# Attention loop reordered: projections one group ahead, assembly, memory update and output projection cut up among the QK steps, private PSUM banks, and five copies moved between ScalarE and VectorE

## The chip, the cores and the metric

One core of a Trainium2 chip. The metric is the device time of one execution in microseconds (us), as the median of several runs. The program on one core has executions that agree within some tenths of a per cent; runs more than 1.5% above the fastest of the same kernel are marked slow and are not used for ratios. Engines: PE (TensorE matmul; PEld is its weight load), ACT (ScalarE), DVE (VectorE), POOL, SP. Each engine is given its own list of instructions, in program order, and the engines wait for one another by semaphores.

## The reference, cut to what matters

```python
# x: 2048 x 640 bf16.  32 heads of 20; 4 segments of 512 rows.
for s in range(4):
    p = softmax(q_s k_s^T * scale + mask)     # causal within the segment
    a_dot = p @ v_s
    a_mem = (phi(q_s) @ M) / (phi(q_s) @ z + 1e-6)
    o_s = g * a_mem + (1 - g) * a_dot
    M, z = M + phi(k_s)^T v_s, z + sum(phi(k_s))
a = concat(o_s) @ wo
out = gate * a + (1 - gate) * b               # b: a 2D FFT filter of x ("part B")
```

`phi(t)` is `t + 1` for `t > 0` and `exp(t)` otherwise, so the q and k projections are needed twice: as they are, for QK, and through phi. The memory (M, z) goes from segment to segment.

## The kernel before

The kernel first computes part B (to about 330 us), then v for all rows (to 381 us), and then runs a loop over 4 segments x 8 groups of four heads. Only this loop, and the v stage a little, is touched. Every operation is recorded in program order by one helper, which puts a semaphore wait in front of it where a buffer needs one; PSUM banks are such buffers and are always exclusive. The parts that matter (cut):

```python
def proj_group(s, g):                  # q into PSUM bank 6, k into bank 7
    for which, ..., bank in (("q", ..., 6), ("k", ..., 7)):
        5 matmuls of 128x512 -> bank
        dve: qT or kT <- bank                     # copy, bf16
        act: pq or pk <- exp(bank)
        dve: rq <- max(qT, 0);  pq <- min(pq, 1) + rq

def qk_unit(s, g, j):                  # j = 0..3: keys of block j, queries from block j on
    for pair in range(2):              # two heads at a time; banks 0..5: three pair slots
        b0 = 2 * (pairctr[0] % 3)
        2 matmuls, 32 rows, N = 512 - 128 j;  2 mask matmuls 128x128
        act: expT <- exp(banks b0, b0 + 1)

def assembly(s, g):                    # bank 6 + g % 2 and bank 7 - g % 2
    PV: 40 matmuls of 22 columns;  4 matmuls pq x Mz_bf;  8 small dve operations -> o_sb

def m_update(s, g):                    # bank 6 + g % 2
    pe: 4 transposes of pk;  act: pkT <- bank;  4 matmuls pkT x v
    dve: 4 x (Mz_acc += bank; memset);  act: Mz_bf <- Mz_acc

def out_proj(s, i):                    # banks 6 and 7
    pe: 5 transposes of o_sb;  act: oT <- bank;  10 matmuls;  dve: outt;  dma

for s in range(NSEG):
    proj_group(s, 0)
    for ui, (g, j) in enumerate(units):
        if j == 0:
            if g + 1 < NG: proj_group(s, g + 1)
            if s <= 2: m_update(s, g)
            if pending_out: out_proj(*pending_out.pop(0))
        qk_unit(s, g, j)
        ...                            # assembly(s, g) two units after the group's last QK
    ...                                # rest of the assemblies; then four output tiles are pending
```

So one group is: projection of the next group, memory update, perhaps an output tile, all through banks 6 and 7, and then four QK steps.

## Time and profile before

| | us |
|---|---|
| median of 12 runs | 893.71 (891.36 to 895.69) |
| first QK matmul of the loop (timeline) | 390.9 |
| mean of a group, first QK to next first QK, 31 intervals | 15.2 |
| mean granted PE clock in the loop (0.5 or 1.0 at any moment) | 0.67 |

The page of the kernel before: busy time of the engines; busy tenths of PE and ACT and the granted PE clock in tenths, in 40 slices; and the shares of the chain of work that ended last.

```profile
span 893.4 us, 10954 instructions
...
PE 599.0 (67%) x4314; PEld 279.0 (31%) x4314; DVE 397.5 (44%) x1050; ACT 326.1 (37%) x530; POOL 16.6 (2%) x46
...
PE   0500799706967664867787776778677768786894
...
ACT  0494012201211113245455343455244355354661
...
PEclk9855599957987876976655757665668665669757
...
PE 54%; DVE 24%; ACT 14%; issue 4%; SPq 2%; DMA 1%; DVEq 0%; ACTq 0%
```

The loop begins at slice 17. PE is at 6 to 8 tenths there (9 once, and 4 in the last slice), ACT at 2 to 6 (1 in the last), and the clock row stands mostly at 5 to 7. DVE is busy 44% of the span. No engine is full. The next two fences are the waits of ACT and of PE within the loop: who waited for whom, us in total, times, longest.

```profile
ACT pq L922 <- DVE qT L921: 75.7, 30, 6.3
ACT expT L953 <- PE psum L270: 63.7, 57, 3.9
ACT Mz_bf L1022 <- DVE Mz_acc L1020: 55.9, 24, 2.5
```

```profile
PE psum L270 <- ACT pkT L1010: 32.5, 24, 2.1
PE psum L270 <- ACT expT L953: 22.2, 32, 1.8
PE psum L1008 <- ACT pk L922: 17.6, 9, 2.4
```

These are chains between engines. The timeline shows one of them (start us, us, engine, operation, and in brackets the idle time before it and who ended it):

```profile
712.38 1.26 PE L270 MATMUL psum<-xT,wk_pad 128*128 128x512 bf16 x5
...
712.60 0.69 DVE L921 CAST qT<-psum 128x512 bf16<-128x512 f32 x1 [1.89 <-PE psum L270]
713.32 0.60 ACT L922 ACTIVATE pq<-psum 128x512 bf16<-128x512 f32 x1 [2.39 <-DVE qT L921]
...
715.85 0.59 ACT L1010 ACTIVATE pkT<-psum 128x512 bf16<-128x512 bf16 x1
...
716.50 0.33 PE L270 MATMUL psum<-vaug,pkT 128*128 128x88 bf16 x4 [2.12 <-ACT pkT L1010]
...
718.69 0.31 ACT L1022 ACTIVATE Mz_bf<-Mz_acc 128x128 bf16<-128x128 f32 x1 [2.25 <-DVE Mz_acc L1020]
718.91 1.01 ACT L953 ACTIVATE expT<-psum 128x1024 bf16<-128x1024 f32 x1
```

While the k projection runs (712.38) qT is copied by DVE (712.60), then follow the exp of q on ACT (713.32, after ACT had idled 2.39 us for qT), the same for k, the pkT copy of the memory update on ACT (715.85), for which the PE waits 2.12 us (716.50), and at last the Mz_bf copy (718.69).

The last view is the busy time in chosen windows (us; the columns are the engines' busy time with the number of instructions, then the clock). The first line is 60 us of the loop, the others are successive windows of 3.41 us:

```profile
395.00:455.00 60.00, 47.87 (x378) 21.00 (x379) 22.26 (x68) 31.77 (x54) 0.00 (x0) 0.61 0.00 1
722.64:726.06 3.42, 3.42 (x18) 1.35 (x19) 2.10 (x7) 1.91 (x4) 0.00 (x0) 0.50 0.00 0
726.06:729.47 3.41, 2.89 (x7) 0.76 (x5) 2.15 (x4) 0.60 (x1) 0.00 (x0) 0.50 0.00 0
729.47:732.88 3.41, 1.82 (x18) 0.92 (x18) 2.02 (x8) 1.19 (x2) 0.00 (x0) 1.00 0.00 0
732.88:736.30 3.42, 2.06 (x35) 1.18 (x36) 0.53 (x4) 2.65 (x4) 0.00 (x0) 0.50 0.00 0
```

The clock is 0.50 or 1.00 for a whole window and never between. The Trainium skill, "TensorE: Matmul & The Clock Gate", Part 1, says that the PE's clock is gated to half by default, that activity opens the gate, and that this is decided per window of about 3.4 us. The trace agrees: each change in it lies on one grid of 3.413 us.

### The profile page before, as it was taken

Reading aid. Unit: us, or ns where it says so; the run is one execution under the profiler, and the core shown is the slowest. Engines: PE = TensorE matmul, PEld = TensorE weight load, DVE = VectorE, ACT = ScalarE, POOL = GpSimd, SP = SyncE. Lnnn points to the kernel's source line nnn. Section 1 sums busy time; section 2 is a strip of 40 time slices with the busy share of each in tenths; the row PEclk is TensorE's granted clock in tenths of the full one; section 3 lists DMA queues with packets and bytes.
Section 4 is the critical chain, followed back from the end, with each engine's and each line's share of the span. In section 5 each row is a group of like instructions: output and inputs, shape, how many; then the busy total and the mean of one; then the engine's idle time right before and its main releaser. Section 6 shows DMA issues by size and latency. Waiting matters only on the chain.

```text
span 893.4 us, 10954 instructions
## 1 busy us (share of the span) xinstructions
PE 599.0 (67%) x4314; PEld 279.0 (31%) x4314; DVE 397.5 (44%) x1050; ACT 326.1 (37%) x530; POOL 16.6 (2%) x46
## 2 busy tenths in 40 slices
PE   0500799706967664867787776778677768786894
PEld 0400244303433322423333333333233333333442
DVE  0476513796243433243433434444524444535542
ACT  0494012201211113245455343455244355354661
POOL 5000000000000000010000000000000000000000
PEclk9855599957987876976655757665668665669757
DMA  9800000000000031000000000000000000000000
GB/s 234 143 0 0 0 1 1 1 0 0 1 1 1 0 111 37 1 1 1 1 1 1 8 8 8 8 1 1 0 16 8 8 1 1 1 15 8 9 1 30
DMA packets 29936, 15.00 MB, mean 17 GB/s; under 512 B 23228, under 2 KB 29884, under 8 KB 29884
## 3 DMA queue, kind: packets, MB, share of 16 engines
q1 hardware_dynamic: 27248, 11.01, 5.2%
q10 hardware_dynamic: 2636, 3.28, 1.1%
q8 instruction: 34, 0.56, 0.2%
q14 instruction: 18, 0.15, 0.1%
HBM read 5.90 MB, written 2.62 MB: 10 GB/s over the span
## 4 chain that ended last, share of the span: by engine, by line
PE 54%; DVE 24%; ACT 14%; issue 4%; SPq 2%; DMA 1%; DVEq 0%; ACTq 0%
PE psum L270 52%; ACT expT L953 4%; DVE pq L924 2%; DVE qT L921 2%; DVE kT L921 2%; ACT pq L922 2%; SPq L124 2%; DVE t L438 2%; ACT pkT L1010 2%; DVE Mz_acc L1019 1%; ACT pk L922 1%; ACT t L443 1%; ACT oT L1034 1%; DVE Mz_acc L1020 1%; DVE prod L613 1%
## 5 line engine op out<-in xcount | busy, mean ns | idle before, releaser
L953 ACT ACTIVATE expT<-psum 128x1024 bf16<-128x1024 f32 (+3 forms) x256 | 165.8, 707 | 67.8 <-PE psum L270 65.7
L270 PE MATMUL psum<-qT,kT 32*128 32x256 bf16 (+3 forms) x512 | 102.1, 395 | 22.5 <-ACT expT L953 22.2
L270 PE MATMUL psum<-maskT,ident 128*128 128x128 bf16 x512 | 92.7, 278 | 0.0
L270 PE MATMUL psum<-xT,wq_pad 128*128 128x512 bf16 x160 | 64.3, 558 | 8.9 <-DVE mtmp L999 6.9
L921 DVE CAST qT<-psum 128x512 bf16<-128x512 f32 x32 | 22.1, 690 | 72.2 <-PE psum L270 72.2
L270 PE MATMUL psum<-xT,wk_pad 128*128 128x512 bf16 x160 | 52.4, 471 | 2.6 <-ACT pk L922 2.6
L983 DVE RECIPROCAL rs<-psum 128x16 f32<-128x16 f32 x32 | 8.2, 258 | 101.6 <-PE psum L270 101.6
L270 PE MATMUL psum<-wo_sb,oT 128*128 128x512 bf16 (+1 forms) x160 | 41.6, 439 | 16.1 <-ACT oT L1034 16.1
L270 PEld LDWEIGHTS psum<-maskT,ident 128*128 128x128 bf16 x512 | 32.0, 105 | 59.1 <-issue 50.4
L922 ACT ACTIVATE pq<-psum 128x512 bf16<-128x512 f32 x32 | 19.1, 597 | 77.1 <-DVE qT L921 77.1
L270 PEld LDWEIGHTS psum<-qT,kT 32*128 32x128 bf16 x512 | 25.7, 97 | 67.5 <-ACT expT L953 32.9
L270 PE MATMUL psum<-x_sb,Jsel 128*128 128x512 bf16 (+1 forms) x16 | 6.7, 459 | 53.4 <-DVE xm L506 53.4
L1044 DVE SCALAR_TENSOR_TENSOR outt<-psum,g_sb,yk 128x512 bf16<-128x512 f32 (+1 forms) x32 | 17.6, 551 | 53.4 <-PE psum L270 52.8
L270 PE MATMUL psum<-vaug,expT 128*128 128x22 bf16 x1280 | 39.9, 180 | 0.0
L270 PEld LDWEIGHTS psum<-vaug,expT 128*128 128x128 bf16 x1280 | 39.4, 104 | 0.2
L270 PE MATMUL psum<-wv_aug,xT 128*128 128x512 bf16 (+1 forms) x160 | 28.4, 328 | 15.9 <-ACT gB L889 11.4
L270 PE MATMUL psum<-cC,Xlr 128*128 128x512 bf16 (+1 forms) x48 | 14.1, 344 | 34.5 <-DVE Xlr L634 34.5
L922 ACT ACTIVATE pk<-psum 128x512 bf16<-128x512 f32 x32 | 19.1, 597 | 46.6 <-DVE kT L921 46.6
L720 ACT ACTIVATE yk<-psum 128x512 bf16<-128x512 f32 (+1 forms) x16 | 6.8, 425 | 78.2 <-PE psum L270 78.2
L270 PE MATMUL psum<-vaug,pkT 128*128 128x88 bf16 x96 | 9.5, 239 | 32.5 <-ACT pkT L1010 32.5
L704 DVE TENSOR_SCALAR uvt<-psum,omg 128x512 f32<-128x512 f32 (+1 forms) x16 | 8.7, 546 | 49.7 <-PE psum L270 49.7
L270 PEld LDWEIGHTS psum<-xT,wk_pad 128*128 128x128 bf16 x160 | 19.4, 124 | 36.0 <-issue 23.9
(209 smaller groups left out, 916.7 us busy)
## 6 DMA issues: line engine op xcount, KB each, us to landing
x_sb<-in_A_x_dram SPq DMA_DIRECT2D x1, 2560.0 KB, 10.0
out_dram<-outt SPq DMA_DIRECT2D x16, 160.0 KB, 1.8
wst<-in_A_wq_dram ACTq DMA_DIRECT2D x1, 800.0 KB, 4.8
wst<-in_A_wk_dram ACTq DMA_DIRECT2D x1, 800.0 KB, 6.6
wo_sb<-in_A_wo_dram ACTq DMA_DIRECT2D x1, 800.0 KB, 8.2
wst<-in_A_wv_dram ACTq DMA_DIRECT2D x1, 800.0 KB, 4.6
xT<-in_A_x_dram SPq DMA_TRANSPOSE x5, 5.3
WrT<-in_B_w_r_dram SPq DMA_TRANSPOSE x3, 5.3
```

The source lines that it names most:

```text
L124: h = eng.dma_start_transpose(out_ap, in_ap)
L270: return e.matmul(out_ap, lhsT, rhs, start=start, stop=stop, tile_position=tile_position)
L438: self.run("dve", lambda e: e.scalar_tensor_tensor(gt[:, 0:n], zt[:, 0:n], -TWO23, u_t[:, 0:n], ALU.add, ALU.subtract), r=[tagz, tagu], w= ...
L443: self.run("act", lambda e: e.activation(at[:, 0:n], gt[:, 0:n], ACT.Abs), r=[tagg], w=[taga])
L613: self.run("dve", lambda e, xa=xa, wa=wa, slot=slot: e.tensor_tensor(pr[slot], xa, wa, ALU.mult), r=rX + rW, w=[f"prod{slot}"])
L921: self.run("dve", lambda e, o_ps=o_ps, dstT=dstT, g=g: e.tensor_copy(dstT[:, g, :], o_ps), r=[pb[bank]], w=[A(tn)])
L922: self.run("act", lambda e, o_ps=o_ps, dstP=dstP, g=g: e.activation(dstP[:, g, :], o_ps, ACT.Exp), r=[pb[bank]], w=[A(pn)])
L924: self.run("dve", lambda e, dstP=dstP, g=g, rb=rb: e.scalar_tensor_tensor(dstP[:, g, :], dstP[:, g, :], 1.0, rb[:, :], ALU.min, ALU.add), ...
L953: self.run("act", lambda e, in_ap=in_ap, out_ap=out_ap: e.activation(out_ap, in_ap, ACT.Exp, scale=SC), r=[pb[b0], pb[b0 + 1]], w=[A(f"{ex ...
L1010: self.run("act", lambda e, pt=pt: e.activation(pt[:, :, :], psbf[:, tb * 1024:tb * 1024 + 4 * P].rearrange("p (a b) -> p a b", b=P), ACT. ...
L1019: self.run("dve", lambda e, dst=dst, src=src: e.tensor_tensor(dst, dst, src, ALU.add), r=[pb[tb]], w=[A("Mz_acc")])
L1044: self.run("dve", lambda e, o_ps=o_ps, c0=c0, cw=cw: e.scalar_tensor_tensor(ot[:, c0:c0 + cw], o_ps, gsb[:, st:st + 1], yk[:, st, c0:c0 + ...
```

## The change

The intent is to keep ACT and PE fed all the time: the projection of the next group, q and k apart, is put between the QK steps of this one, the assembly and the memory update of the previous group and an output tile likewise, and this goes on across segment ends. Each user has its own banks: QK 0 to 3 (two pair slots in place of three), PV 4, Mz and transposes 5, q 6, k 7 (an output tile's matmuls borrow 6 and 4, the memory product 7). qT and kT are evacuated by ACT; pkT, oT and Mz_bf by DVE. oT is now tracked tile by tile and no longer as one buffer of four tiles. The core of the diff (cuts marked; renamed banks and debug lines left out):

```diff
-                eng = "act" if (st + ci) % 2 == 0 else "dve"      # v stage
-                if eng == "act":
+                if ci == 0:
...
-                self.run("dve", lambda e, ...: e.tensor_copy(dstT[:, g, :], o_ps), ...)
+            self.run("act", lambda e: e.activation(dstT[:, g, :], o_ps, ACT.Copy), ...)
...
-                b0 = 2 * (pairctr[0] % 3)
+            b0 = 2 * (pairctr[0] % 2)
...
-            self.run("act", lambda e, pt=pt: e.activation(pt[:, :, :], psbf[...], ACT.Copy), ...)
+            self.run("dve", lambda e: e.tensor_copy(pt[:, :, :], psbf[...]), ...)
...
-            self.run("act", ... e.activation(Mz_bf[nb][:, g, :], Mz_acc[:, g, :], ACT.Copy), ...)
+            self.run("dve", ... e.tensor_copy(Mz_bf[nb][:, g, :], Mz_acc[:, g, :]), ...)
...
+        groups = [(s, g) for s in range(NSEG) for g in range(NG)]
+        proj_full(0, 0)
+        for gi, (s, g) in enumerate(groups):
+            nxt, prv = ...                       # across segment ends
+            upd = prv is not None and prv[0] <= 2
+            qk_pair(s, g, 0, 0); qk_pair(s, g, 0, 1)
+            if prv: assembly(*prv); ...          # four output tiles pending at a segment's end
+            qk_pair(s, g, 1, 0); qk_pair(s, g, 1, 1)
+            if nxt: proj_mm(*nxt, "q"); proj_copy, proj_exp, proj_dve(*nxt, "q"); proj_mm(*nxt, "k")
+            qk_pair(s, g, 2, 0); qk_pair(s, g, 2, 1)
+            if pending_mm: out_mm(*pending_mm.pop(0), b512=6, b128=4)
+            if upd: m_update(*prv)               # transposes of pk, pkT
+            if nxt: proj_copy, proj_exp, proj_dve(*nxt, "k")
+            qk_pair(s, g, 3, 0); qk_pair(s, g, 3, 1)
+            if pending_out: out_tr(...); pending_mm.append(...)
+            if upd: m_update_b(*prv)             # pkT x v, Mz_acc, Mz_bf
+        ...                                      # last assembly; last four tiles through all eight banks
```

## The prediction

> **What bounds the kernel now.** Only the attention loop (382 to 870 us of 893; by the timeline) is changed. It runs 32 groups (segment, four heads) at about 15.3 us each. By the group view, a group needs ACT about 7.5 us (eight exps back to back took 5.02 us; two 512-column exps at 0.60 each; small copies), DVE about 9 us, PE about 8 us at full clock but 12.4 us at half clock (five 512-column matmuls 1.27 or 2.34 us; one head pair with its two masks 0.54 or 0.86 us). No engine is full: in the timeline the projection, its evacuation (CAST 0.69, exp 0.60), the pk transposes, the pkT copy, the Mz product and out_proj follow one another between groups. PE waits there about 5 us and ACT 4 to 7 us; ACT's waits for qT total 77 us, PE's for pkT and oT 49 us.
>
> Second bound: the clock. In the windows view it is 0.5 or 1.0 only, changing on a 3.41 us grid, mean about 0.65 in the loop. The Trainium skill, "TensorE: Matmul & The Clock Gate", Part 1, says that activity in such a window releases the throttle; the trace agrees. Adding matmul columns x rows/128 per grid window, nearly every window above about 0.38 of the full-rate array was followed by clock 1.0 and those below by 0.5. So idle gaps shorter than a window count too; 32-row QK, and PV with 22 columns, count little.
>
> **What the change does.** The projection moves one group ahead, q and k between j steps; assembly, memory update and out_proj are cut up among the QK steps of the next group, and go on across segment ends; every user has its own PSUM banks (QK keeps two pair slots instead of three). qT/kT evacuation goes from DVE (0.69) to ACT (about 0.6); pkT, oT and Mz_bf from ACT to DVE. Work is almost unchanged: ACT about 7.7 us per group, DVE 7.5 (9.4 with out_proj), PE 7.8 (9.7) at full clock. Nothing much is removed: the gain is overlap.
>
> **Cost.** Laying these durations along the new order by hand gives, at full clock, 8.8 us per group and 10.3 with out_proj: 298 us for the loop. I don't expect full clock. Between two projections lie 6.6 us of QK/PV/transposes whose activity is about 0.35 to 0.4, just at the threshold, so windows without a projection or out_proj will often turn the clock to 0.5, and a projection will turn it back. Expected: 10.5 us for plain groups, about 11.5 with out_proj, mean clock in the loop 0.7 to 0.8, 346 us in all, PE the bound. Fill 5 us; the tail shrinks from 23 to about 19 us because eight banks are used. Everything before 382 us is unchanged, but for 1 us in the vaug stage.
>
> 381 + 5 + 346 + 19 = 751 us. I say **750 us**, 80% range **710 to 798** (full clock throughout 701; half clock throughout about 825). Faster by over 2%: 0.95; within 2%: 0.03; slower: 0.02.
>
> **What would show it.** Groups view: DVE's wait qT<-PE and ACT's wait pq<-DVE vanish; PE's waits for pkT and oT shrink below 10 us each. Windows: PE busy over 90% in the loop; clock still flips in 3.41 us steps. Chain of waits: the DVE share falls, PE's grows, with ACT exp steps. Busy time of ACT and DVE about unchanged in total.
>
> **What would make it wrong.** The interleave keeps every window above the threshold: then 700 to 715. Or in-order queues couple badly: DVE late (pkT copy queued behind outt, Mz behind pk), PE waiting for two QK slots or bank 5: then groups of 12 to 13 us, about 800.

## The result, and the profile after

| | before | after |
|---|---|---|
| median, us | 893.71 (12 runs) | 720.42 (8 runs, 719.24 to 723.41) |
| ratio of fast runs | 1 | 0.8065 (95%: 0.8052 to 0.8079) |
| first QK matmul of the loop, us | 390.9 | 382.9 |
| 31 group intervals, us | 471.4 | 312.9 |
| last group's first QK to the end, us | 31.2 | 23.2 |
| mean clock in the loop | 0.67 | 0.87 |

A ratio is the mean time of one kernel's fast runs over the mean of the other's fast runs in the same rounds, so it is not quite the ratio of the medians quoted. Rows 3 to 5 are worked out from the start times of QK matmuls in the two traces; their differences, 8.0 + 158.4 + 8.0, make up the 174.4 us between the two profiled spans. By segment the intervals went from 118.9, 137.6, 133.0 and 81.9 us (7 intervals in the last) to 83.5, 82.1, 78.6 and 68.7 us. The last segment has no memory update, and there the old order lost least.

The same lines of the page after:

```profile
span 719.0 us, 11006 instructions
...
PE 521.9 (73%) x4314; PEld 260.2 (36%) x4314; DVE 369.6 (51%) x1048; ACT 335.2 (47%) x532; POOL 16.6 (2%) x46
...
PE   0510079995149768663687988899989999899986
...
ACT  0089301121003111102426677667877678768871
...
PEclk9999999998559987885797788889978999879976
...
PE 62%; DVE 17%; ACT 13%; issue 3%; SPq 2%; DMA 1%; DVEq 0%; ACTq 0%
```

PE's row is at 8 and 9 in the loop (slices 22 to 38), ACT's at 6 to 8. DVE's share of the chain fell and PE's grew. The waits of PE and of ACT in the loop, the same views as before:

```profile
PE psum L275 <- ACT pk L933: 11.7, 16, 0.8
PE psum L275 <- ACT expT L974: 5.6, 10, 1.1
...
PE psum L275 <- DVE pkT L1027: 0.8, 2, 0.4
```

```profile
ACT expT L974 <- PE psum L275: 52.4, 86, 1.7
ACT qT L928 <- PE psum L275: 22.4, 18, 1.3
```

PE's wait of 32.5 us for pkT is 0.8 us now, the wait of ACT for qT, 75.7 us, and for the Mz additions, 55.9 us, are gone; what ACT now waits for is the PE. Some PE lines of segment 2 (timeline):

```profile
575.53 1.52 PE L275 MATMUL psum<-wo_sb,oT 128*128 128x512 bf16 x10
576.89 0.39 PE L1025 MATMUL psum<-ident,pk 128*128 128x128 bf16 x4
...
578.42 0.45 PE L1052 MATMUL psum<-ident,o_sb 128*128 128x128 bf16 x5 [0.38 <-DVE pkT L1027]
578.71 0.32 PE L275 MATMUL psum<-vaug,pkT 128*128 128x88 bf16 x4
...
582.13 1.24 PE L275 MATMUL psum<-xT,wq_pad 128*128 128x512 bf16 x5
583.22 1.24 PE L275 MATMUL psum<-xT,wk_pad 128*128 128x512 bf16 x5
```

The output tile (575.53), the pk transposes (576.89), the o_sb transposes (578.42), the Mz product (578.71) and both projections (582.13, 583.22) stand in one stream, with QK steps and PV in the cut lines between them and one wait of 0.38 us. In the stretches that the kernel before spent waiting, QK steps now run.

The windows after: 60 us of segment 0, then four successive windows in it; and two windows in segment 2:

```profile
395.00:455.00 60.00, 54.70 (x532) 26.78 (x530) 26.48 (x91) 42.80 (x69) 0.00 (x0) 0.81 0.01 2
438.54:441.96 3.42, 3.42 (x10) 1.24 (x10) 0.77 (x2) 2.17 (x4) 0.00 (x0) 0.50 0.00 0
441.96:445.37 3.41, 2.59 (x23) 1.15 (x21) 1.41 (x3) 2.18 (x5) 0.00 (x0) 1.00 0.01 2
445.37:448.78 3.41, 2.98 (x58) 1.99 (x58) 2.44 (x11) 2.76 (x6) 0.00 (x0) 1.00 0.00 0
448.78:452.20 3.42, 3.42 (x11) 1.25 (x10) 0.67 (x3) 2.15 (x3) 0.00 (x0) 0.50 0.02 5
```

```profile
571.66:575.08 3.42, 3.42 (x23) 1.48 (x22) 3.04 (x11) 2.96 (x5) 0.00 (x0) 1.00 0.00 0
575.08:578.49 3.41, 3.03 (x30) 1.70 (x30) 2.25 (x5) 2.97 (x7) 0.00 (x0) 1.00 0.00 0
```

In segment 0 the clock goes half, full, full, half, again and again. A group there takes 10.2 us (the last six intervals: 10.20, 10.22, 10.22, 10.49, 10.17, 10.23), and three windows are 10.24 us: the loop has locked to the clock's grid. In segment 2 (the last two lines), where groups 1 to 4 carry an output tile, the clock stays full from 564.8 to 609.2 us, and three of these groups, though they have more work, take 9.62, 9.62 and 9.35 us.

### The profile page after: what moved, and what is told of

Its sections match the earlier page's. It is cut to its first block, busy times and chain, and to the rows that moved or that the text cites. A ratio compares the mean times of both kernels' runs of the same rounds, so it can differ in the third digit from the quotient of the medians.

```text
span 719.0 us, 11006 instructions
## 1 busy us (share of the span) xinstructions
PE 521.9 (73%) x4314; PEld 260.2 (36%) x4314; DVE 369.6 (51%) x1048; ACT 335.2 (47%) x532; POOL 16.6 (2%) x46
## 4 chain that ended last, share of the span: by engine, by line
PE 62%; DVE 17%; ACT 13%; issue 3%; SPq 2%; DMA 1%; DVEq 0%; ACTq 0%
PE psum L275 61%; ACT expT L974 3%; SPq L129 2%; DVE t L443 2%; ACT t L448 2%; DVE prod L618 1%; ACT kT L928 1%; ACT pk L933 1%; ACT vaug L908 1%; DVE thr L717 1%; DVE yk L711 1%; DVE uvt L709 1%; DVE xm L511 1%; DVE uvt L714 1%; ACT Sq L446 1%
## 5 line engine op out<-in xcount | busy, mean ns | idle before, releaser
L275 PE MATMUL psum<-qT,kT 32*128 32x256 bf16 (+3 forms) x512 | 83.5, 323 | 10.8 <-ACT expT L974 5.6
L275 PE MATMUL psum<-maskT,ident 128*128 128x128 bf16 x512 | 77.1, 235 | 0.0
L275 PE MATMUL psum<-xT,wq_pad 128*128 128x512 bf16 x160 | 58.8, 517 | 0.3 <-ACT vaug L908 0.3
L275 PE MATMUL psum<-wv_aug,xT 128*128 128x512 bf16 (+1 forms) x160 | 28.4, 328 | 15.3 <-ACT gB L894 11.4
L940 DVE TENSOR_SCALAR rq<-qT 128x512 bf16<-128x512 bf16 x32 | 10.4, 324 | 42.2 <-ACT qT L928 42.2
L556 ACT ACTIVATE XST<-psum 128x512 bf16<-128x512 f32 (+2 forms) x13 | 6.5, 499 | 52.2 <-PE psum L275 43.6
L928 ACT ACTIVATE qT<-psum 128x512 bf16<-128x512 f32 x32 | 19.1, 597 | 24.4 <-PE psum L275 23.8
L275 PE MATMUL psum<-Fr,Cq 128*128 128x128 bf16 (+1 forms) x128 | 29.9, 390 | 0.0
L941 DVE SCALAR_TENSOR_TENSOR pq<-pq,rq 128x512 bf16<-128x512 bf16 x32 | 22.2, 692 | 13.2 <-ACT pq L933 13.2
L672 ACT ACTIVATE Fr<-psum 128x512 bf16<-128x512 f32 x8 | 4.8, 597 | 47.4 <-PE psum L275 47.4
L941 DVE SCALAR_TENSOR_TENSOR pk<-pk,rq 128x512 bf16<-128x512 bf16 x32 | 22.2, 692 | 9.1 <-ACT pk L933 8.6
```

The source lines that it names most:

```text
L275: return e.matmul(out_ap, lhsT, rhs, start=start, stop=stop, tile_position=tile_position)
L928: self.run("act", lambda e: e.activation(dstT[:, g, :], o_ps, ACT.Copy), r=[pb[bank]], w=[A(f"{which}T{g}")])
L940: self.run("dve", lambda e: e.tensor_scalar(rb[:, :], dstT[:, g, :], 0.0, None, ALU.max), r=[A(tn)], w=[A(rbn)])
L941: self.run("dve", lambda e: e.scalar_tensor_tensor(dstP[:, g, :], dstP[:, g, :], 1.0, rb[:, :], ALU.min, ALU.add), r=[A(rbn)], w=[A(pn)])
```

## The experiments

All were run against the kernel before in the same rounds; ratios are to that kernel, and the kernel after stands at 0.8065. What follows is in two parts: which part of the change made the gain, and what the clock has to do with it.

For the second part I use a score, worked out from the traces: for each window of the grid, the sum over its matmuls of the time that their columns need at the granted clock, times rows/128, times the granted clock, as a share of the window. (A column takes about 0.42 ns at full clock: in the timeline of segment 2 above, ten matmuls of 3200 columns in all start at 575.53 and what follows them starts at 576.89.) So 1 is the array fully used at full clock, and 0.5 is the most that half clock allows. In the loops of before and after (247 windows from 380 us on), a score of at least 0.374 was followed by clock 1.0 and a lower one by 0.5 in all but 6; over all 14 profiles, in all but 58 of 1579. The threshold was chosen to fit, so this is a description and not a test; the tests are below. A rival description fails: if a window is judged by the share of it in which the PE is busy, even the best threshold misjudges 413 of the 1579.

### Engine moves alone

```diff
 # the kernel before, same order and banks
-  dve: qT, kT      act: pkT, Mz_bf, oT
+  act: qT, kT      dve: pkT, Mz_bf, oT
```

> The kernel before, its order and PSUM banks kept, with only the engine moves: qT/kT evacuation to ACT, pkT, oT and Mz_bf to DVE. Theory (the gain is the new order, the engine moves only balance it): the same chain of waits stays, 875 to 900 us. Rival (the engine moves carry much of the gain): below 850 us.

Measured: 859.59 us median, ratio 0.9594 (0.9522 to 0.9665). Both theories missed a little: more than "nothing", far from "much".

### New order alone

```diff
 # the kernel after, new order and banks
-  act: qT, kT      dve: pkT, Mz_bf, oT
+  dve: qT, kT      act: pkT, Mz_bf, oT (but for the last four output tiles, as in after)
```

> The kernel after with the engines of before (qT/kT evacuation on DVE, pkT, oT, Mz_bf on ACT), new order and banks kept. Theory (order carries the gain): 730 to 765 us, so at least three quarters of the 173 us. Rival (engine moves carry much): above 800 us.

Measured: 788.38 us, ratio 0.8807 (0.8784 to 0.8829). Between the two expectations. The order alone is worth 11.9%, the moves alone 4.1%, together 19.4%: the moves are worth more in the new order than in the old. The next run shows where most of that lies. (The order here comes with its PSUM banks and the finer tracking of oT; what these two bring by themselves was not run apart.)

### One copy moved back

```diff
 # the kernel after
-  self.run("dve", ... e.tensor_copy(Mz_bf[nb][:, g, :], Mz_acc[:, g, :]), ...)
+  self.run("act", ... e.activation(Mz_bf[nb][:, g, :], Mz_acc[:, g, :], ACT.Copy), ...)
```

> The kernel after with one instruction per group of the first three segments moved back: the 128x128 copy Mz_bf on ACT instead of DVE. It waits for the four Mz additions on DVE, and ACT runs in order, so the first exps of the next group wait behind it, about 2 us. Theory (queue order on ACT): 24 x 1.5 to 2 us more, 755 to 770 us, that is most of what the run with all four engine moves undone lost. Rival (evacuation of qT and kT on ACT is what counted): below 735 us.

Measured: 774.02 us, ratio 0.866 (0.8647 to 0.8673), a little above the range expected. So 24 copies of 0.31 us each, on the wrong queue, cost 54 us of the 720, and they are most of the 68 us that all the moves cost when undone. ACT's waits in that run, and its timeline at one group's end:

```profile
ACT Mz_bf L1044 <- DVE Mz_acc L1042: 55.2, 24, 2.9
```

```profile
442.48 0.31 ACT L1044 ACTIVATE Mz_bf<-Mz_acc 128x128 bf16<-128x128 f32 x1 [1.98 <-DVE Mz_acc L1042]
442.69 2.79 ACT L974 ACTIVATE expT<-psum 128x1024 bf16<-128x1024 f32 x3
```

The copy needs the last of four Mz additions on DVE. ACT idles 1.98 us for it, and only then comes to the exps of the next group (442.69), though their inputs need no Mz_bf. The Trainium skill, "TensorE: Matmul & The Clock Gate", Part 1, "Architectural detail", says that ACT and DVE take their queues strictly first in, first out; here that order costs 55.2 us in 24 waits. The kernel before shows the same 55.9 us, but there it was one wait among several, and how much of the 34 us of the first experiment is due to it was not run apart. The mean clock in the loop fell too, from 0.87 to 0.78, so part of the 54 us may be PE time at half clock that the waits brought on; the run does not part the two.

### The pipeline drained at segment ends

```diff
-            nxt = groups[gi + 1] if gi + 1 < len(groups) else None
-            prv = groups[gi - 1] if gi > 0 else None
+            nxt = (s, g + 1) if g + 1 < NG else None
+            prv = (s, g - 1) if g > 0 else None
...
+            if g == NG - 1 and s < NSEG - 1:
+                assembly(s, g); pending_out.extend(...); m_update(s, g); m_update_b(s, g)
+                proj_full(s + 1, 0)
```

> The kernel after, but the pipeline is drained at each of the three segment ends (assembly, memory update and the first projection of the next segment stand alone there). In the trace of before, a segment end cost about 6 us more than the mean group. Theory: 3 x 6 to 10 us, so 738 to 750 us. Rival (carrying the pipeline across segment ends matters little, the order within the segment is all): 718 to 728 us.

Measured: 737.44 us, ratio 0.8248 (0.8219 to 0.8277): 17 us for three segment ends, 0.6 us under the range expected. Carrying on across segment ends is a tenth of the gain; the rest is within the segment.

### Output projections left out

```diff
 # the kernel after; WRONG result on purpose
-                    pending_out.extend((prv[0], i) for i in range(4))
+                    for i in range(4):  # part B goes out as it is
+                        self.dma("sp", self.out2[...], yk[:, st_, :], ...)
```

> The kernel after without the output projections of segments 0 to 2 (wrong result on purpose: the B part goes out in their place). They take some 20 us of PE at full clock in 12 groups. Theory A (the clock follows array activity, and out_proj keeps it at 1.0 where it stands): these groups become plain groups of 10.2 us with a clock near 0.8, and the time stays within 8 us of the kernel after, or grows. Rival B (groups are bound by the PE's work): 15 to 22 us less, about 700 us.

Measured: 726.43 us, ratio 0.813 (0.8105 to 0.8155). Twelve output tiles less, and the kernel is 0.8% slower than with them. The group intervals say how: in segments 1 to 3 they are now 10.2 us nearly without exception (10.22, 10.22, 10.22, 10.23, 10.24, 10.24 at the end of segment 1), three clock windows each, and the mean clock of the loop fell from 0.87 to 0.82. The rival, that a group's time is its work, expected some 20 us less. It falls.

### Two and four useless matmuls in the plain groups

```diff
+        def dummy(n):
+            for _ in range(n):
+                self.mm(ps[:, 6*512:7*512], self.ident[:], self.xT[:, 0, 0:512], start=True, stop=True, ...)
...
             if prv: assembly(*prv) ...
+            if plain: dummy(1)          # plain: no output tile in this group.  In the second run 2
...
             if upd: m_update_b(*prv)
+            if plain: dummy(1)          # in the second run 2
```

> The kernel after with two 512-column matmuls of no use (into a free PSUM bank) added to every group that has no output projection: one after the PV stage, one at the group's end. Right result. Theory A (clock follows array activity per 3.41 us window): plain groups stay at clock 1.0 and fall from 10.2 us to about 9.2 us, so 700 to 708 us. Rival B (PE work bounds the groups): about 0.43 us more in 19 groups, 728 us.

> The same with four such matmuls per plain group, two at each place. Theory A: if two were enough, the two more cost up to 0.43 us per plain group, 705 to 714 us; if two were not enough, this one is the faster. Rival B: 737 us.

Measured: 724.18 us, 0.8091 (0.8042 to 0.814), and 722.15 us, 0.8079 (0.8048 to 0.8109). Neither theory's number; not to be told from the kernel after. The trace of the first of them shows one thing that went wrong. One of its windows:

```profile
453.14:456.56 3.42, 2.52 (x27) 1.26 (x25) 2.17 (x7) 2.72 (x6) 0.00 (x0) 1.00 0.00 0
```

In segment 0 some groups did fall to 8.83 us, but every second one took 11.4 us or more. The window at 453.14, busy for 2.52 of its 3.42 us, scored 0.35 and was followed by half clock: it holds the third and fourth QK steps, the transposes and the wait for the exp of k, and my extra matmul came after that wait. I had filled two places of a group and left the third.

In the run with four the clock did rise. Its loop from first to last group:

```profile
384.65:693.02 308.37, 287.11 (x3038) 145.48 (x3039) 185.82 (x603) 231.33 (x373) 0.00 (x0) 0.92 0.02 8
```

The mean clock is 0.92 where the kernel after has 0.87, and yet the time is the same. At full clock a plain group of segments 0 to 2 took 9.25 to 9.55 us here, and 8.62 to 8.68 us in the kernel after: the added matmuls cost about what the clock gave. So a raised clock alone is not a gain; it counts where the work that raises it stands.

### The same, in the right place

```diff
             if pending_mm: out_mm(...)
+            if plain: dummy(3)          # where the other groups have their output tile
             if upd: m_update(*prv)
...                                      # and dummy(1) after the assembly
```

> The kernel after with four useless 512-column matmuls in each group without an output projection, as in the four-matmul run, but three of them where the output projection stands in the other groups (after the third QK step, ahead of the wait for the pk exp) and one after PV. Theory A, with the place corrected (the windows that turned to half clock in the two earlier runs held the third and fourth QK step): plain groups fall to 8.6 to 9.2 us, 695 to 706 us. If this too stays at 718 to 726 us, the activity of the window is not what holds the clock down, or cannot be mended so.

Measured: 707.58 us, ratio 0.7921 (0.7896 to 0.7945): 1.8% faster than the kernel after, with four more matmuls in each plain group and the right result; just outside the range expected. Mean clock in the loop 0.92 against 0.87. Not every group stays at full clock: segment 0 has 8.62 us groups and some of 10.1 to 11.6. Its loop, and PE's wait for the exp of k (us in total, times, longest) from 380 to 690 us, first in the run with four at the other places, then here:

```profile
383.07:683.87 300.80, 281.15 (x3008) 148.75 (x3039) 184.99 (x603) 231.86 (x373) 0.00 (x0) 0.92 0.03 8
```

```profile
PE psum L275 <- ACT pk L933: 11.7, 16, 0.8
PE psum L275 <- ACT pk L933: 5.8, 13, 0.7
```

So the same four matmuls give nothing or 13 us, depending on where they stand; but the mean clock is 0.92 in the profiles of both runs, so what parts these two is not the mean clock. It is what the matmuls cost: at full clock a plain group takes 8.62 to 8.93 us here, hardly more than in the kernel after. Three of the four now stand ahead of a wait that the PE had anyway, and that wait became shorter. Against the kernel after, both hold: the clock is up, and the work that holds it up is nearly free.

### The output work spread evenly

```diff
-                out_mm(...)             # a tile, 512 + 128 columns, in groups 1 to 4
+                out_half(...)           # 320 columns in every group; transposes in every second one
```

> The kernel after with the same output projections spread evenly: half a tile (320 columns) in each group of segments 1 to 3, in place of whole tiles in groups 1 to 4. Same work. Theory A: all groups of segments 1 to 3 stay near clock 1.0 and take about 9.1 us, 200 to 215 us for them in place of 229 us: 700 to 708 us. Rival B: unchanged, 717 to 723 us.

Measured: 706.16 us, ratio 0.7904 (0.7886 to 0.7922): 2.0% faster than the kernel after with the same arithmetic. Of the sixteen group intervals in segments 1 and 2, twelve are 8.62 to 8.68 us, and one alone is above 10.1 (12.57). Mean clock in the loop 0.90. Not all of the 14 us is the clock: at full clock a group with half a tile takes as long as a plain one in the kernel after (8.62 to 8.68 us), while six groups with a whole tile took 9.34 to 9.62 there, some 5 us more in all. How the rest divides was not run apart.

### Both together

```diff
 # the kernel with half tiles
+            if plain or s == 3: dummy(1)    # after the assembly
...
+            if plain: dummy(3)              # after the third QK step
```

> The kernel with half an output tile per group (706 us) with three useless 512-column matmuls after the third QK step of the groups that have no half tile (mostly segment 0), and one after PV there and in segment 3. Right result. Theory A: segment 0 falls from 84 to 70 us, segment 3 from 66 to about 61 us: 688 to 696 us. Rival: no gain, 706 us or more.

Measured: 698.55 us, ratio 0.781 (0.779 to 0.7829): right result, the fastest of all, 3.2% under the kernel after (0.781/0.8065), but 2.5 us above the range that I expected: segment 0 came to 77.6 us in place of 70 and segment 3 gained nothing (67.4 against 66.2 us). Window from 480 to 540 us, first this kernel, then the kernel after:

```profile
480.00:540.00 60.00, 58.12 (x668) 32.92 (x671) 46.25 (x157) 50.18 (x83) 0.00 (x0) 0.97 0.03 10
```

```profile
480.00:540.00 60.00, 56.78 (x618) 30.33 (x619) 42.33 (x141) 45.21 (x72) 0.00 (x0) 0.90 0.04 13
```

PE, ACT and DVE all do more in the same 60 us, at a clock of 0.97 in place of 0.90.

### The old order with the clock kept up

```diff
 # the kernel before; m_update, and in the second run qk_unit too
+            dummy(4)                        # 3 in the second run
             transposes of pk ...
+            dummy(4)                        # 3 in the second run
             4 matmuls pkT x v ...
...
+        second run: 1 and 3 such matmuls ahead of the two pairs of the second QK step
+        segment 3, after the projection: dummy(4)    # 3 in the second run
```

> The kernel before with eight useless 512-column matmuls per group where the PE waits (ahead of the pk transposes and ahead of the Mz product; four per group in the last segment). Theory A (half clock is a good part of what before loses): mean clock in the loop from 0.67 to above 0.85, groups from 14.3 to 12 to 13 us, 825 to 860 us. Rival (only the waits matter): no faster than 890 us, and up to 50 us slower for the added work.

> The kernel before with useless matmuls at every place where its PE waits in a group: three ahead of the pk transposes, three ahead of the Mz product, one and three ahead of the two pairs of the second QK step. Theory A (half clock is a good part of what before loses): mean clock in the loop above 0.88 and 820 to 855 us. Rival (before loses by its waits, and the clock alone gives little): 870 us or more even at such a clock.

Measured: 880.86 us, ratio 0.9839 (0.9794 to 0.9885), and 876.72 us, ratio 0.9732 (0.9672 to 0.9792). The first lies between the two theories, and by the 2% limit it is unclear whether it is faster at all. In the second, two of four runs were marked slow, the profiled one among them; the two fast ones are 865.21 and 874.44 us at a mean clock of 0.840 and 0.824 over the execution, where the kernel before has 0.721 to 0.761 in the same rounds. Its clock in the loop missed the 0.88 that I had asked for (0.83 in the profile, which is of a slow run). So a clock that comes near the one of the kernel after (0.822 to 0.871 over its eight executions; 0.87 in its loop) brought the old order 2.7%, of the 19.4%. (The clock over a whole execution takes in the part before the loop, where it differs from run to run of the same kernel, so the loop's 0.83 is the better figure.) The added matmuls may cost time too, as they did in the runs above, so the clock may be worth more than this there; what it would be without them was not run. In the old order the PE still stood idle for 81 of the loop's 455 us in the second run's profile (114 of 471 in the kernel before).

## Why the prediction was right or wrong

The range (710 to 798 us) held 720.4; the middle was 30 us too high. No errors cancelled: nearly every term was too high. The twelve groups with an output tile took 120 us where 138 were forecast, the other twenty some 200 in place of 210, fill and tail 6 us less. Step by step:

- **"No engine is full: ... follow one another between groups"; the gain is overlap: right.** PE's waits for pkT and ACT's for qT went as named. The order alone brought 11.9%, a raised clock in the old order 2.7%. The step I did not see is that the engine moves are not only a balance: "pkT, oT and Mz_bf from ACT to DVE" hides a 54 us effect in Mz_bf alone, through queue order (and what that did to the clock). I had costed it as 0.3 us of work.
- **First QK at 386, measured 382.9; tail 19, measured 15.8** (703.3, end of the last exp, to 719.0). Both right in direction and 3 us too slow. The v stage gained 1.6 us (the fill of ones that waits for its end starts at 379.2 in place of 380.8) where I said 1.
- **Plain groups "10.5 us": right.** 10.2 us in most of segment 0, with the clock at 0.5 in one window of three. I had no idea that it would lock to the grid.
- **"About 11.5 with out_proj": wrong, and this is the term that was mis-sized.** After a first long interval in each segment (11.94, 12.23, 12.60), these groups took 9.54, 9.55, 9.34; 9.62, 9.62, 9.35; and 8.72, 8.73, 8.72. The twelve average 10.0. Two reasons are seen, and one of them was tested. The clock: I let out_proj share the half-clock windows of plain groups, but its 3200 columns lift the very windows that would have failed; the run without output tiles shows this. And the DVE, by my own sums: I took 0.69 us for the pkT copy, which is the measured time of the copy from f32 PSUM, but the transposes leave bf16 in PSUM, and it took 0.42 us (oT, 640 columns: 0.48). The Trainium skill, "VectorE: DVE Perf Modes", "Why PSUM operands drop a tier", says that a PSUM operand still allows a doubled rate, but not when it is fp32; the trace agrees, 0.42 against 0.69 us for 512 columns. So my 10.3 us at full clock was 0.7 to 1.0 us too much in segments 1 and 2 before the clock came in (1.6 in segment 3, which has no memory update). That the two copies explain this is argued and was not run.
- **Mean clock "0.7 to 0.8": too low**, 0.87, for the same reason. **"PE busy over 90%": right**, 54.70 and 55.01 us of 60 in the windows at 395 and 515 us. **ACT's and DVE's total busy time about unchanged: right for ACT** (326.1 to 335.2 us), DVE fell from 397.5 to 369.6.
- **"What would make it wrong", late DVE or too few QK slots:** PE's waits for exps are 5.6 us in the loop and for bank 5 some 3 us. Two slots were enough.

What stays open: why some groups still fall to half clock in the fastest kernel (mostly in segments 0 and 3). In segment 0 the windows that turned it to half scored 0.32 to 0.35, so the rule agrees; why these windows hold less than those of other groups with the same work was not followed up.

## What to carry to other kernels

ScalarE took its queue in order here (24 waits of 55.2 us in all before one copy), so a copy that waits long should stand on the queue of the engine that it waits for, or behind the work that needs nothing from it: one copy of 0.3 us per group cost 2 us of idle ScalarE per group. When the PE's clock is 0.5 in some windows of a loop that looks busy, count columns x rows per 3.41 us window, and spread the dense matmuls so that each window gets some; taking work out may gain nothing, and adding work may gain if it stands where the engine waits anyway; elsewhere it costs what it gains. When costing a moved operation, look at its own dtype and memory, not at those of the operation it replaces.

## What the Trainium skill lacked or had wrong

- "TensorE: Matmul & The Clock Gate", "Why this matters for your kernels", advises against idle gaps of more than about 3 us. Here the clock went to half after windows in which the PE was busy for 2.98 of 3.41 us (445.37 in the kernel after). What fits 1521 of 1579 windows is columns x rows/128 at or above about 0.37 of the full-rate window. Matmuls of 32 rows thus count a quarter, which the page does not say: with that weight the best threshold misjudges 53 windows, and 306 if they count in full.
- The same page, Part 4, says that transposes do not count as PE activity in the same way. Here 101 windows of the 14 profiles reach 0.374 only by their transposes, and 100 of them were followed by full clock; of 221 windows without transposes that score 0.30 to 0.374, 29 were. With the transposes left out of the score, the best threshold misjudges 151 of 1579 windows in place of 53. Two windows of the kernel before show it: 654.4 with 0.35 and no transposes was followed by half clock, 674.9 with 0.34 and 0.06 from transposes by full clock. So these transposes count. The trace lists them as MATMUL and does not show whether they run in the mode that the page means.
- No page has it: a loop whose period is near a whole number of clock windows can lock to them. Groups took 10.2 us against 3 x 3.413 = 10.24 us, in segment 0 of the kernel after and in all of segments 1 to 3 when the output tiles were taken out.
